# Two stages change places among the first products, the first keys come through a second queue, and the filler multiplies ones

## The chip, the cores and the metric

The kernel runs on one core of a Trainium2 chip. A core has five engines that work at the same time, each with its own queue of instructions: TensorE (matrix products and transposes, PE in the profile; its weight loads are listed as PEld), VectorE (DVE), ScalarE (ACT), GpSimd (POOL) and SyncE (SP), which here only issues transfers between the chip's memory and the core's. The metric is device microseconds (us) from the first to the last instruction; the time of a kernel is the median of its runs.

## The reference

The kernel computes a retention block (attention with decaying weights instead of a softmax) and feeds it to a two-layer network with the activation h * erf(softplus(h)):

```python
B, H, S, D = 8, 8, 576, 64
scores = (q @ k.transpose(0, 1, 3, 2)) / sqrt(D)          # per batch and head
gamma  = 1 - 2.0 ** (-5 - arange(H))
Dmat   = where(i >= j, gamma ** (i - j), 0)                # i query position, j key position
attn   = (scores * Dmat) @ v                               # (B, H, S, D)
x      = attn.transpose(0, 2, 1, 3).reshape(4608, 512)     # tokens x 512

h   = x @ w_in                                             # 4608 x 2048
g   = h * erf(softplus(h))
out = g @ w_out                                            # 4608 x 512
```

The weights come as 64-bit floats and are rounded to 32 bits on the chip; all else is 32-bit floats.

## The kernel before

The 4608 tokens are cut into 36 attention blocks of 128 and into 9 chunks of 512 (four blocks each). Attention block i has three stages, in the text T, S and O with the block's number:

```python
def transposes(i):                       # T: queries and keys, on TensorE through PSUM
    ...
    for name in "qk":
        ...
            pt = ps_at.tile([P, NP, P], FP32, tag="at", name=f"pt_{name}")
            for p in range(NP):
                nc.tensor.transpose(pt[:, p, :], flat(t[name][:, 2 * p : 2 * p + 2, :]), ident)
            ...
                nc.scalar.copy(out=tT, in_=pt)          # ScalarE takes them out of PSUM
    load(i + 2, "q")

def scores(i):                           # S: q k^T, then the mask, on VectorE
    ...
            nc.tensor.matmul(ps[e][:, p, :], lhsT=t["kT"][...], rhs=t["qT"][...], ...)
    for e in range(2):
        tt(sT[:, e], ps[e], mask..., ALU.mult)

def outputs(i):                          # O: masked scores x values, running state; needs sT
    ...
    load(i + 3, "kv")
```

From block 8 on the queries are transposed by VectorE (`raw_qs`), and only the keys go through TensorE and ScalarE. The first chunk's product with w_in is cut into 16 steps, which the loop below calls `p`: for each of four slices of the 512 inputs, four products (tiles p, p, pe, pg), each of which grows over the slices. The last four end with a copy by ScalarE:

```python
def plain(self):
    acc = [ps_a.tile([P, W], FP32, tag="a", name=f"p{n}") for n in range(2)]
    acc += [ps_e.tile([P, W], FP32, tag=n, name="p" + n) for n in "eg"]
    ...
    for dc in range(n_dc):                                  # 4 slices
        for n in range(4):                                  # p, p, pe, pg
            ...
                nc.tensor.matmul(acc[n]..., lhsT=wa[...], rhs=t[...], ...)
            if dc == n_dc - 1:
                nc.scalar.copy(out=(self.t2 if tok else self.t1)[:, f], in_=acc[n])
            yield

def softplus(self): ...    # ScalarE, two activations of 128x1024
def erf(self): ...         # ScalarE, two activations of 128x1024
```

A weight tile arrives in two transfers (w_in) or one (w_out) and is rounded in five steps: two activations on ScalarE (L250, L251), then VectorE (L255, L259, L263, and L268 to L271; for w_out GpSimd takes the last two). Each slice of the products needs one rounded w_in tile.

All engines run in program order. The start of the program is written as one string, a letter a stage: `a` the next attention stage, `p` the next product step, `w` the transfer of a weight tile, a digit that many rounding steps, `k` two filler products, `l`, `c` and `s` transfers. A filler is a product of the identity with itself whose result nobody reads; it keeps TensorE from idling:

```python
idle = ps_e.tile([P, W], FP32, tag="g", name="idle")
def keep_busy(n):
    for _ in range(n):
        nc.tensor.matmul(idle[:, :P], lhsT=ident, rhs=ident, start=True, stop=True)
...
keep_busy(9)
weigh_values(0)
products = firsts[0].plain()
for what in "alkakakawkakakawaa3awwa2aaa5ppappawwppa5ppawapp5wcppa5ppaaapp5s":
    ...
firsts[0].softplus()
firsts[0].erf()
attend(after_chunk(1))                                      # O7
store_x(1)
for step, _ in enumerate(firsts[1].plain()):                # the next chunk's products
    if step % 2 == 0:
        attend(min(done[0] + 1, most[0]))                   # T8, S8, T9, O8, ...
    round_weights(int(step > 1))
    ...
```

Written out from the first product on (pp is two product steps; numbered pp1 to pp8), the string before gives: pp1 T5 pp2 O4 ww pp3 S5 5 pp4 O5 w T6 pp5 5 w c pp6 S6 5 pp7 T7 O6 S7 pp8 5 s, and then softplus, erf, O7.

Of the kernel before, what the change touches and what calls it, by code (L numbers as in the profile page):

```python
# [11 lines left out]
FP32 = mybir.dt.float32  # L12
# [6 lines left out]
P = 128  # L19
# [35 lines left out]
def kernel(  # L55
# [10 lines left out]
    nc = tc.nc  # L66
# [15 lines left out]
    cpool = ctx.enter_context(tc.tile_pool(name="cpool", bufs=1))  # L82
# [21 lines left out]
    heads = [slice(e * D, (e + 1) * D) for e in range(2)]  # L104
# [18 lines left out]
    def load_squares(i, name, src):  # L123
        t = raw.tile([P, NP, P * D // SQ], FP32, tag=name + "s", name=f"raw_{name}s", bufs=2)
        for b, s0, n, r0 in pieces[i]:
            m = n // SQ * D
            for part in range(P // SQ):
                e, d0 = part // 2, part % 2 * SQ
                tokens = src[b, e * NP : (e + 1) * NP, s0 : s0 + n, :].rearrange("p (r a) d -> r p (a d)", r=SQ)
                at = r0 // SQ * D  # L130
                nc.sync.dma_start(
                    out=t[part * SQ : (part + 1) * SQ, :, at : at + m - SQ], in_=tokens[:, :, d0 : d0 + m - SQ]
                )
        return t

    def load_rows(i, name, src, bufs):
        if name == "q":
            t = raw.tile([P, NP, P * D // SQ], FP32, tag="qs", name="raw_q", bufs=bufs)
            t = t.rearrange("p a x -> p (a x)")[:, : H * D].rearrange("p (h d) -> p h d", h=H)
        else:  # L140
            t = raw.tile([P, H, D], FP32, tag=name, name=f"raw_{name}", bufs=bufs)
        for b, s0, n, r0 in pieces[i]:
            for e in range(2):
                heads = src[b, e * NP : (e + 1) * NP, s0 : s0 + n, :]
                nc.sync.dma_start(out=t[r0 : r0 + n, e::2, :], in_=heads.rearrange("h p d -> p h d"))  # L145
        return t

    def load(i, names="qkv"):
        if i < len(pieces):
            t = loaded.setdefault(i, {})  # L150
            for name in names:
                src = {"q": q, "k": k, "v": v}[name]
                if name == "q" and i < SQUARES:
                    t["q"] = load_rows(i, "q", q, 2)
                elif name == "q":
                    t["qs"] = load_squares(i, "q", q)
                    if i >= SQUARES_K:
                        t["ks"] = load_squares(i, "k", k)
                elif name == "v" or i < SQUARES_K or len(pieces[i]) == 1:
                    t[name] = load_rows(i, name, src, 4)  # L160

    load(0)
    cst = cpool.tile([P, CONST_COLS], FP32, name="cst")
    nc.sync.dma_start(out=cst[:, :CONST_FIRST], in_=consts[:, :CONST_FIRST])
# [63 lines left out]
    def load_weights():  # L228
        part = next(coming, None)
        if part is not None:  # L230
            t = wraw.tile([P, 2 * WP], UINT32, tag="wraw", name="wraw")
            for rows, src in part[0]:
                nc.sync.dma_start(out=t[rows].rearrange("p (h f) -> p h f", h=2), in_=src)
            words.append((t, *part[1:]))
# [49 lines left out]
    def round_weights(n=1):  # L284
        for _ in range(n):
            next(round_step, None)

    ident = cpool.tile([P, P], FP32, name="ident")
# [13 lines left out]
    def weigh_values(i):  # L302


        if i < len(pieces) and i not in weighed:
            weighed.add(i)
            t = (loaded.get(i) or live[i])["v"]
            by = gk if len(pieces[i]) == 1 else gk2
            nc.gpsimd.tensor_tensor(out=t, in0=t, in1=by.unsqueeze(2).to_broadcast([P, H, D]), op=ALU.mult)
# [136 lines left out]
    def attend(upto):  # L446
        while done[0] < min(upto, len(stages)):
            of, i = stages[done[0]]
            of(i)
            done[0] += 1  # L450
# [9 lines left out]
    def store_x(c):  # L460
        nc.sync.dma_start(out=xd[c], in_=x[0, c][:, :n_dc])
# [240 lines left out]
    idle = ps_e.tile([P, W], FP32, tag="g", name="idle")  # L702

    def keep_busy(n):
        for _ in range(n):
            nc.tensor.matmul(idle[:, :P], lhsT=ident, rhs=ident, start=True, stop=True)  # L706


    most = [before_chunk(2)]
# [1 line left out]
    def run(steps, rounds=(), stages=1):  # L711

        for step, _ in enumerate(steps):
            attend(min(done[0] + stages, most[0]))
            round_weights(rounds[step] if step < len(rounds) else 0)

    keep_busy(9)
    weigh_values(0)
    products = firsts[0].plain()

    for what in "alkakakawkakakawaa3awwa2aaa5ppappawwppa5ppawapp5wcppa5ppaaapp5s":
        if what == "a":
            attend(done[0] + 1)
        elif what == "p":
            next(products)
        elif what == "s":
            store_x(0)
        elif what == "l":  # L730
            load(2, "kv")
        elif what == "c":
            nc.sync.dma_start(out=cst[:, CONST_FIRST:], in_=consts[:, CONST_FIRST:])
        elif what == "w":
            load_weights()
        elif what == "k":
            keep_busy(2)
        else:
            round_weights(int(what))
# [17 lines left out]
    for b, nxt in zip(blocks[2:], blocks[3:] + [None]):  # L757
        n = order.index((b.g, b.c))
# [73 lines left out]
```

## Time and profile before

| | before |
|---|---|
| time, median of 3 runs | 1032.35 us (1030.36 to 1032.41) |
| span of the profiled execution | 1030.6 us |
| busy: TensorE, VectorE, ScalarE, GpSimd | 1018.5, 666.8, 390.2, 122.4 us |
| granted TensorE clock, mean | 0.998 |
| SyncE issues transfers without a break | 0.73 to 16.72 us |
| first filler, first transposes on TensorE | 1.36, 5.36 us |
| first weight tile: issued, landed | 16.72, 23.5 us |
| ScalarE: table loads, softplus and erf of the first chunk | 60.59 to 67.20 us |

A line of the profile names the engine, the line of the kernel, the operation, the tile written and the tiles read, and the shape; x16 is the number of instructions. In brackets stands how long the engine stood idle before it and what ended the wait. A query of a stretch of time gives, for each engine, the busy time, and beside it the clock that TensorE was granted (1.00 is full speed) and the mean busy share of the 16 DMA engines. [...]

### The profile page before, as it was taken

Reading aid. Unit: us, or ns where it says so; the run is one execution under the profiler, and the core shown is the slowest. Engines: PE = TensorE matmul, PEld = TensorE weight load, DVE = VectorE, ACT = ScalarE, POOL = GpSimd, SP = SyncE. Lnnn points to the kernel's source line nnn. Section 1 sums busy time; section 2 is a strip of 40 time slices with the busy share of each in tenths; the row PEclk is TensorE's granted clock in tenths of the full one; section 3 lists DMA queues with packets and bytes.
Section 4 is the critical chain, followed back from the end, with each engine's and each line's share of the span. In section 5 each row is a group of like instructions: output and inputs, shape, how many; then the busy total and the mean of one; then the engine's idle time right before and its main releaser. Section 6 shows DMA issues by size and latency. Waiting matters only on the chain.

```text
span 1030.6 us, 15945 instructions
## 1 busy us (share of the span) xinstructions
PE 1018.5 (99%) x6346; PEld 877.0 (85%) x6346; DVE 666.8 (65%) x1054; ACT 390.2 (38%) x481; POOL 122.4 (12%) x122
## 2 busy tenths in 40 slices
PE   8989999999999999999999999999999999999998
PEld 7778888888788888888888888888888888888887
DVE  2858877777876666666566666666667655555555
ACT  2354133232244544334343344444443333333332
POOL 2233121222311110000001001100100000000000
PEclk9999999999999999999999999999999999999999
DMA  9996979979984444444445344444433334444433
GB/s 187 210 249 141 238 166 241 236 167 247 225 193 148 165 143 143 143 158 166 160 145 174 138 143 145 159 167 143 143 123 123 123 126 129 131 134 131 125 90 115
DMA packets 146986, 165.76 MB, mean 161 GB/s; under 512 B 97376, under 2 KB 121568, under 8 KB 138848
## 3 DMA queue, kind: packets, MB, share of 16 engines
q1 hardware_dynamic: 145904, 163.96, 56.0%
q8 instruction: 50, 0.82, 0.3%
q10 hardware_dynamic: 1008, 0.79, 0.3%
q14 instruction: 24, 0.20, 0.1%
HBM read 117.52 MB, written 47.19 MB: 160 GB/s over the span
## 4 chain that ended last, share of the span: by engine, by line
PE 95%; DVE 1%; ACT 1%; SPq 1%; DMA 1%; issue 0%; POOL 0%; POOLq 0%; ACTq 0%; DVEq 0%
PE a L600 24%; PE a L492 23%; PE g L600 12%; PE g L492 12%; PE e L600 6%; PE e L492 6%; PE s L343 3%; PE o L361 3%; PE o L384 2%; PE o L372 1%; PE p L546 1%; PE pg L546 1%; SPq L145 1%; DMA wraw<-in_moe_w_in_dram 1%; PE pe L546 1%; PE idle L706 0%
## 5 line engine op out<-in xcount | busy, mean ns | idle before, releaser
L492 PE MATMUL a<-x,wa 128*128 128x256 f32 x1088 | 258.3, 380 | 0.0
L492 PEld LDWEIGHTS a<-x,wa 128*128 128x128 f32 x1088 | 205.7, 190 | 28.5
L600 PE MATMUL a<-wb,s 128*128 128x256 f32 x864 | 205.7, 381 | 0.0
L600 PEld LDWEIGHTS a<-wb,s 128*128 128x128 f32 x864 | 162.9, 190 | 23.6 <-ACT o L614 0.7
L99 DVE TENSOR_TENSOR t<-g,t 128x512 f32<-128x512 f32 x68 | 47.0, 691 | 150.4 <-ACT t L522 113.2
L492 PE MATMUL g<-x,wa 128*128 128x256 f32 x544 | 129.2, 380 | 0.0
L492 PEld LDWEIGHTS g<-x,wa 128*128 128x128 f32 x544 | 102.8, 190 | 14.4
L99 DVE TENSOR_TENSOR o<-a,o 128x512 f32<-128x512 f32 x108 | 74.1, 686 | 49.3 <-PE a L600 49.3
L517 ACT COPY t<-a 128x512 f32<-128x512 f32 x34 | 19.9, 585 | 188.2 <-PE a L492 188.2
L99 DVE TENSOR_TENSOR t<-t,s 128x1024 f32<-128x1024 f32 x72 | 88.4, 1268 | 0.0
L561 ACT ACTIVATE s<-t 128x1024 f32<-128x1024 f32 x72 | 72.1, 1049 | 27.4 <-DVE t L99 27.4
L270 POOL TENSOR_TENSOR wraw<-wraw 128x512 f32<-128x512 f32 x28 | 29.4, 1051 | 443.3 <-DVE wraw L268 185.9
L99 DVE TENSOR_TENSOR x<-x 128x512 f32<-128x512 f32 x115 | 75.7, 692 | 1.2
L528 ACT COPY t<-a 128x512 f32<-128x512 f32 x34 | 19.9, 586 | 144.3 <-PE a L492 144.3
L565 ACT ACTIVATE s<-s 128x1024 f32<-128x1024 f32 x72 | 72.1, 1048 | 0.4
L99 DVE TENSOR_TENSOR sT<-s,cst 128x512 f32<-128x512 f32 x72 | 46.1, 681 | 35.4 <-PE s L343 35.4
L600 PE MATMUL g<-wb,s 128*128 128x256 f32 x288 | 68.6, 381 | 0.0
L600 PE MATMUL e<-wb,t 128*128 128x256 f32 x288 | 68.5, 380 | 0.0
L600 PE MATMUL a<-wb,t 128*128 128x256 f32 x288 | 68.5, 380 | 0.0
L600 PE MATMUL g<-wb,t 128*128 128x256 f32 x288 | 68.2, 380 | 0.0
L99 DVE TENSOR_TENSOR o<-g,o 128x512 f32<-128x512 f32 x72 | 49.2, 684 | 24.8 <-ACT o L614 20.0
L492 PE MATMUL e<-x,wa 128*128 128x256 f32 x272 | 64.8, 381 | 0.0
(75 smaller groups left out, 1226.0 us busy)
## 6 DMA issues: line engine op xcount, KB each, us to landing
od<-o SPq DMA_DIRECT2D x54, 512.0 KB, 3.3
x<-xd SPq DMA_DIRECT2D x27, 1024.0 KB, 4.8
o<-od SPq DMA_DIRECT2D x27, 1024.0 KB, 5.2
raw_qs<-in_q_dram SPq DMA_DIRECT2D x96, 112.0 KB, 4.5
raw_ks<-in_k_dram SPq DMA_DIRECT2D x84, 112.0 KB, 4.3
xd<-x SPq DMA_DIRECT2D x9, 1024.0 KB, 5.1
raw_k<-in_k_dram SPq DMA_DIRECT2D x64, 128.0 KB, 4.6
raw_v<-in_v_dram SPq DMA_DIRECT2D x64, 128.0 KB, 4.6
```

The costliest lines, as they stand in the source:

```text
L99: nc.vector.tensor_tensor(out=out, in0=in0, in1=in1, op=op)
L270: engine.tensor_tensor(out=r_f, in0=high_f, in1=r_f, op=ALU.mult)
L343: nc.tensor.matmul(ps[e][:, p, :], lhsT=t["kT"][heads[e], p, :], rhs=t["qT"][heads[e], p, :], start=True, stop=True)
L361: nc.tensor.matmul(o[p % 2][heads[(e + p) % 2], p // 2, :], lhsT=t["v"][:, 2 * p + e, :], rhs=t["sT"][:, e, p, :], start=(p < 2), stop=(no ...
L384: nc.tensor.matmul(kv[heads[e], p, :], lhsT=t["k"][:, 2 * p + e, :], rhs=t["v"][:, 2 * p + e, :], start=False, stop=(p == NP - 1), skip_gr ...
L492: nc.tensor.matmul(acc[:, j * TH : (j + 1) * TH], lhsT=weights["wa", self.g][:, a, d, j * P : (j + 1) * P], rhs=x[self.g, self.c][a][:, d, :],
L517: nc.scalar.copy(out=self.t1[:, 1], in_=self.a)
L528: nc.scalar.copy(out=self.t2[:, 0], in_=self.a)
L546: nc.tensor.matmul(acc[n][:, j * TH : (j + 1) * TH], lhsT=wa[:, slots[f], dc % 2, j * P : (j + 1) * P], rhs=t[:, dc, tok * TH : (tok + 1) ...
L561: nc.scalar.activation(self.s[:, j], t, AF.Softplus)
L565: nc.scalar.activation(self.s[:, j], self.s[:, j], AF.Erf)
L600: nc.tensor.matmul(acc[:, tp, :], lhsT=left[:, j * TH + tp * P : j * TH + (tp + 1) * P], rhs=weights["wb", self.g][:, b, j, :], start=(sta ...
```

## The change

It has three parts. The first pair of transfers of keys is issued by ScalarE, beside the queries on SyncE's queue, so that SyncE's queue is two issues shorter. The filler multiplies a tile of ones that VectorE writes, which does not have to wait for GpSimd's identity, and there are ten at the start instead of nine. And two stages change places in the string: T6 moves from before pp5 to behind it, and pp8 moves from behind O6 and S7 to ahead of them, so that the last products of the first chunk, and with them its copies and its softplus, come earlier.

```diff
         for b, s0, n, r0 in pieces[i]:
             for e in range(2):
                 heads = src[b, e * NP : (e + 1) * NP, s0 : s0 + n, :]
-                nc.sync.dma_start(out=t[r0 : r0 + n, e::2, :], in_=heads.rearrange("h p d -> p h d"))
+
+                queue = nc.scalar if (name, i) == ("k", 0) else nc.sync
+                queue.dma_start(out=t[r0 : r0 + n, e::2, :], in_=heads.rearrange("h p d -> p h d"))
@@
+    ones = cpool.tile([P, P], FP32, name="ones")
+    nc.vector.memset(ones, 1.0)
     load(0)
@@
-            nc.tensor.matmul(idle[:, :P], lhsT=ident, rhs=ident, start=True, stop=True)
+            nc.tensor.matmul(idle[:, :P], lhsT=ones, rhs=ones, start=True, stop=True)
@@
-    keep_busy(9)
+    keep_busy(10)
@@
-    for what in "alkakakawkakakawaa3awwa2aaa5ppappawwppa5ppawapp5wcppa5ppaaapp5s":
+    for what in "alkakakawkakakawaa3awwa2aaa5ppappawwppa5ppapp5wawcppa5ppappaa5s":
```

Written out, the string after gives: pp1 T5 pp2 O4 ww pp3 S5 5 pp4 O5 pp5 5 w T6 w c pp6 S6 5 pp7 T7 pp8 O6 S7 5 s, and then as before.

## The prediction

> **What bounds the kernel now.** I read the page first, then the clock of the core, the waits of TensorE, the timeline of the first 85 us, and the chain of waits over the same stretch. The page says where a gain can be at all:
>
> ```profile
> PE 1018.5 (99%) x6346; PEld 877.0 (85%) x6346; DVE 666.8 (65%) x1054; ACT 390.2 (38%) x481; POOL 122.4 (12%) x122
> PE 95%; DVE 1%; ACT 1%; SPq 1%; DMA 1%; issue 0%; POOL 0%; POOLq 0%; ACTq 0%; DVEq 0%
> ```
>
> TensorE is busy in 1018.5 of 1030.6 us and is 95% of the chain that ended last. So only some 12 us of idle time, and time in which TensorE is busy but slow, can be taken away. What the change edits runs in the first 60 us, so I looked for both there and just behind. The list of TensorE's waits has a single large one:
>
> ```profile
> PE s L343 <- ACT kT L334: 3.6, 2, 3.4
> PE p L546 <- DVE wa L271: 1.1, 1, 1.1
> PE pt_k L328 <- DMA raw_k<-in_k_dram: 0.6, 1, 0.6
> ```
>
> The columns are the total in us, how often, and the longest. The timeline shows what stands before the 3.4 us (columns: start, duration, engine, line, operation):
>
> ```profile
> 56.80 0.73 PEld L546 LDWEIGHTS pe<-x,wa 128*128 128x128 f32 x4
> 57.97 0.58 ACT L555 COPY t<-pe 128x512 f32<-128x512 f32 x1 [3.70 <-PE pe L546]
> 58.84 0.59 ACT L555 COPY t<-pg 128x512 f32<-128x512 f32 x1 [0.28 <-PE pg L546]
> 59.32 0.68 ACT L250 ACTIVATE wb<-wraw 128x512 f32<-128x512 f32 x1
> 59.90 0.68 ACT L251 ACTIVATE wraw<-wraw 128x512 f32<-128x512 uint32 x1
> 60.59 1.28 ACT L561 ACT_TABLE_LOAD   x1
> 61.89 2.00 ACT L561 ACTIVATE s<-t 128x1024 f32<-128x1024 f32 x2
> 63.91 1.28 ACT L565 ACT_TABLE_LOAD   x1
> 65.20 2.00 ACT L565 ACTIVATE s<-s 128x1024 f32<-128x1024 f32 x2
> 67.11 0.56 ACT L334 COPY kT<-pt_k 128x512 f32<-128x512 f32 x1
> 67.73 1.30 PEld L343 LDWEIGHTS s<-qT,kT 64*128 64x128 f32 x16 [3.79 <-ACT kT L334]
> ```
>
> The reader is to see an unbroken ScalarE queue from 58.84 to 67.67 us. The transposed keys of attention block 8 wait in PSUM from about 62.5 us, but their copy stands behind two table loads, softplus and erf, and those behind the copies of the last two products of the first block (pe, pg). The scores of block 8 (L343) wait for that copy. The granted clock of the same microseconds shows a second cost (columns: stretch, its length, TensorE busy, clock, DMA share, GB/s):
>
> ```profile
> 66.00:67.00 1.00, 0.00 (x0) 1.00 0.97 402
> 67.00:68.00 1.00, 0.27 (x4) 1.00 0.97 410
> 68.00:69.00 1.00, 1.00 (x16) 0.65 1.07 286
> 69.00:70.00 1.00, 1.00 (x6) 0.50 1.35 238
> 70.00:71.00 1.00, 1.00 (x4) 0.50 1.34 345
> 71.00:72.00 1.00, 1.00 (x4) 0.65 0.97 410
> ```
>
> After that idle time TensorE runs at half clock from about 68.3 to 71.7 us: 3.4 us that do 1.7 us of work.
>
> **What the Trainium skill says.** "TensorE: Matmul & The Clock Gate", section "Part 1: The HAM clock gate", puts the clock at half after about one idle window of 3.4 us, and back at full after about 3.4 us of sustained work, with windows that run free of the kernel's start. The trace agrees: 3.39 us idle, then 3.4 us at half. The same page, under "Architectural detail: the array is 16× 32×32, not 1× 128×128", says that ScalarE and VectorE take their queues strictly in order; the copy that stands 4.6 us behind ready data (62.5 to 67.1) agrees. "DMA: Bandwidth & Descriptors", section "Issuing engines are not separate DMA queues", says that transfers issued by two engines share the same 16 DMA engines, and that a second issuer saves only issue time. In this trace one issue takes SyncE 0.5 us, and the DMA share is already 0.91 at 3.0 to 4.5 us and 1.13 at 4.5 to 6.0, so I expect little from the second queue.
>
> **The change part by part.** I write O for an attention block's outputs, S for its scores, T for its transposes, and pp1 to pp8 for the pairs of products; the number after O, S and T is the block.
>
> *Part 1, order, first half.* T6 moves from before pp5 to behind it. Before, O5 ends at 44.02, T6 follows, pp5 begins at 44.77, just behind VectorE's last rounding step for its weights (L271 at 43.99, 0.69 long, so 44.68). Without T6 ahead TensorE waits 44.68 - 44.02 = 0.7 us. The work between 44.02 and pp7 (T6, pp5, pp6, S6) took 43.95 to 49.58 = 5.63 us and only changes its order, so pp7 can begin at 44.77 + 5.63 = 50.40 instead of 50.68. Its weights must be ready: ScalarE's step for them (L250, at 45.65 behind T6's copies) is now ahead of those copies; VectorE starts behind O5's three multiplications (end 45.67), and needs the 3.59 us of the part before (41.09 to 44.68), so 49.3. The wait of 1.1 us at pp7 goes, one of 0.7 comes: gain 0.3.
>
> *Part 2, order, second half.* pp8 moves from behind O6 and S7 to ahead of them. pp7 50.40 + 1.99 = 52.39; T7 0.88 gives 53.27; pp8 1.94 gives 55.2; O6 2.24 and S7 1.09 give 58.53. Now O7 follows S7 at once, and needs the masked scores: two VectorE multiplications, 1.29 us together, so 58.53 + 1.29 and 0.12 of hand-over, 59.94; pp8 used to hide them. Before, O7 began at 58.73 without waiting, so O7 is now 1.2 us later, and so is everything up to the next chunk's third product (its end was 64.34): 65.55.
>
> ScalarE meanwhile: pg's copy ends at about 55.85 instead of 59.43. Then the same queue as in the fence: 1.26 (L250, L251), 1.28, 2.00, 1.28, 2.00, so erf ends at 63.7; block 8's transposes, also 1.2 us later, end at 63.7 too; their copy ends at 64.3. TensorE reaches S8 at 65.55 and finds it ready. The wait of 3.39 becomes none: S8 begins at 65.55 instead of 67.73, gain 2.2 (part 1's 0.3 is in it). No idle stretch longer than 1.3 us is left, so the clock stays up, and S8, pg and p take 1.09 + 1.06 + 0.86 = 3.0 us as their like do elsewhere, instead of the 72.44 - 67.73 = 4.7 measured: gain 1.7. Together 3.9 us at the transposes of block 9.
>
> *Part 3, the first keys on ScalarE's queue.* It takes two issues, 1.06 us, out of SyncE's queue, which issues without a break from 0.73 to 16.72, and the first weights (issued at 16.72, landed at 23.5) end a wait in the chain. At most 1.06 us, if SyncE alone set the pace; DMA shares of 1.17 to 1.23 from 7.5 to 15 us say that the transfers set it too, while 0.62 and 0.67 at 15.0 to 16.5 and 18.0 to 19.5 leave room. I choose half: 0.5 us. Queries and keys now come in together; the first transposes start at 5.36, behind the filler, and do not need either earlier.
>
> *Part 4, the filler.* It begins at 1.36 now, once GpSimd has built the identity. A tile of ones needs one VectorE memset and should be ready about 0.4 us earlier. One more product (two instructions of 4.21 / 18 = 0.234 us) takes 0.47. It ends where it ended: 0 us, unless the clock rises a window earlier.
>
> Sum: 3.9 + 0.5 = 4.4 us, if all of it reaches the end.
>
> **The rivals.** (a) *The gain is given back later.* DMA is at a share of 1.03 in 150 to 200 us, and at 272 us the chain goes through a transfer of keys (2.68 us) for 0.6 us of TensorE's waiting. If transfers, and not TensorE, set the pace up to 300 us, an earlier TensorE only waits longer, and 2 to 4 us are lost: 1029 to 1032. Against it: the loads are issued as buffers come free, which moves earlier too, and slices with a DMA share of 0.6 and 0.7 lie between. (b) *The wait for masked scores at O7 takes the place of the one removed*, and the clock falls anyway: with a wait of 2 us or more and softplus not hidden, S8 would gain 1 us or nothing: 1030 to 1032. Against it: VectorE's queue is empty at that point, its rounding steps stand behind the masking. (c) *Part 1 costs more than it gains*: if pp5's weights come 1 us later than worked out, 0.7 us is lost. (d) *Queries and keys in two queues delay the first transposes* (the queries alone had landed by about 4.1 us): they have 1 us of slack, so 0 to 0.5 us. (e) SyncE's queue was the bound and all of 1.06 comes through: 1027.4.
>
> **Range and chances.** 1032.35 - 4.4 = 1028.0. For rival (a) I take 0.3 off the gain in the mean: 1028.3. The three times of before spread over 2.05 us (1030.36 to 1032.41), about the cost of one fall of the clock, so a median can lie 1 us off; the full gain with (e) and a lucky start gives 1026.2, most of (a) or (b) gives 1031.3. A change of 2% is 20.6 us; TensorE's total idle time is 12, so faster by that is not to be had, and nothing here could cost as much: 0.99 for within 2%.
>
> **What would show each step.** ScalarE's copies of pe and pg at about 54 to 56 us; the wait of L343 for kT gone from TensorE's list, and a wait of O7 (L361) for VectorE's sT of 1 to 1.5 us in its place; granted clock 1.00 in all of 60 to 80 us; TensorE's wait at the first pp5 instead of pp7; block 9's transposed keys at 68 us or earlier instead of 72.4; SyncE's first weight transfer issued at 16.2 instead of 16.7. I am wrong if TensorE still waits over 2 us before S8, if the clock still falls there, or if block 9 is 4 us earlier and the end is not.

## The result, and the profile after

| | before | after |
|---|---|---|
| time, median of 6 runs | 1032.68 us (1030.36 to 1033.56) | 1027.33 us (1026.85 to 1029.08) |
| span of the profiled execution | 1030.6 us | 1026.7 us |
| ratio, with 95% interval | | 0.9953 (0.9940 to 0.9966) |

A ratio of 0.9953 is 4.9 us less, with an interval of 3.5 to 6.2. The two profiled executions differ by 3.9 us. The page of the changed kernel, busy time of the engines and the chain that ended last:

```profile
PE 1017.5 (99%) x6348; PEld 876.0 (85%) x6348; DVE 669.2 (65%) x1055; ACT 390.2 (38%) x481; POOL 123.5 (12%) x122
PE 95%; DMA 2%; DVE 2%; SPq 0%; issue 0%; ACT 0%; DVEq 0%
```

TensorE remains the bound. It is busy 1.0 us less, although the first filler takes 4.64 us instead of 4.21: here the half clock that is gone shows. The other 2.9 of the 3.9 us were idle time. TensorE's waits of the changed kernel in the first 100 us (the columns are the total in us, how often, and the longest; line numbers are four higher than before):

```profile
PE idle L710 <- DVE ones L165: 1.1, 1, 1.1
PE o L365 <- POOL raw_v L313: 0.8, 1, 0.8
PE p L550 <- DVE wa L275: 0.7, 1, 0.7
PE pt_k L332 <- DMA raw_k<-in_k_dram: 0.7, 2, 0.4
PE s L347 <- ACT kT L338: 0.3, 1, 0.3
PE pt_q L332 <- DMA raw_q<-in_q_dram: 0.2, 1, 0.2
```

The wait of 3.4 us for the copy of block 8's keys has gone. A wait at the outputs (L365) and waits for transfers of keys and queries stand there instead. Behind 100 us one more is listed, for VectorE's transposes of block 31:

```profile
PE s L347 <- DVE kT L326: 0.9, 1, 0.9
```

The kernel before waits 0.6 us at that place. The timeline of the changed kernel around the scores of block 8:

```profile
54.93 0.61 ACT L559 COPY t<-pe 128x512 f32<-128x512 f32 x1
55.41 0.62 ACT L559 COPY t<-pg 128x512 f32<-128x512 f32 x1
...
57.19 1.28 ACT L565 ACT_TABLE_LOAD   x1
57.95 1.29 DVE L99 TENSOR_TENSOR sT<-s,cst 128x512 f32<-128x512 f32 x2 [0.25 <-PE s L347]
58.71 0.19 PEld L365 LDWEIGHTS o<-sT,raw_v 128*64 128x64 f32 x2 [0.99 <-POOL raw_v L313]
...
59.29 0.85 PEld L365 LDWEIGHTS o<-sT,raw_v 128*64 128x64 f32 x14 [0.39 <-DVE sT L99]
...
61.81 2.00 ACT L569 ACTIVATE s<-s 128x1024 f32<-128x1024 f32 x2
...
63.72 0.57 ACT L338 COPY kT<-pt_k 128x512 f32<-128x512 f32 x1
...
64.75 0.97 PEld L347 LDWEIGHTS s<-qT,kT 64*128 64x128 f32 x16 [0.33 <-issue]
...
68.05 0.42 PEld L332 LDWEIGHTS pt_k<-ident,raw_k 128*128 128x128 f32 x4 [0.62 <-issue]
```

ScalarE's copies of pe and pg come about 3 us earlier, so erf ends at 63.8 and the keys' copy at 64.3, before TensorE has got to block 8's scores (64.75, where it was 67.73). O7 waits for its masked scores: its first two weight loads run at 58.71, the other 14 at 59.29, when VectorE has written sT. The lists put the first part of this wait down to GpSimd (raw_v L313), but that ended at 58.21; VectorE's first half of sT ended at 58.64. The granted clock in the stretch that ran at half before:

```profile
68.00:69.00 1.00, 0.92 (x7) 1.00 1.25 405
69.00:70.00 1.00, 1.00 (x6) 1.00 0.97 410
70.00:71.00 1.00, 1.00 (x15) 1.00 0.92 330
```

The clock stays at 1.00. The most useful view is one worked out from these timelines: when TensorE begins the scores of each attention block, less the same of the kernel before (us; less is earlier). The later columns are experiments told below; S15 to S26 stand as S11 in every column.

| scores of block | before, at | after | order alone | pp8 alone | T6 alone | start alone | filler in the wait | copy first |
|---|---|---|---|---|---|---|---|---|
| 1 | 13.90 | -0.97 | +1.64 | -0.76 | -0.29 | -0.87 | -0.08 | -0.83 |
| 4 | 29.64 | -1.42 | +0.72 | -0.89 | -0.77 | -0.92 | -0.77 | -1.46 |
| 5 | 38.69 | -0.36 | +0.86 | -0.44 | -0.40 | -0.32 | -0.30 | -0.67 |
| 7 | 55.71 | +1.05 | +2.27 | +1.29 | -0.72 | -0.38 | -0.29 | -0.73 |
| 8 | 67.73 | -2.98 | -1.76 | -2.74 | -0.71 | -0.37 | -0.27 | -4.03 |
| 9 | 78.11 | -4.17 | -3.39 | -4.36 | -0.65 | -0.40 | -1.89 | -5.52 |
| 11 | 96.91 | -4.17 | -3.39 | -4.36 | -0.65 | -0.40 | -1.89 | -5.52 |
| 30 | 267.09 | -4.17 | -3.39 | -4.37 | -0.66 | +0.18 | -1.90 | -5.24 |
| 31 | 276.59 | -3.81 | -3.99 | -4.64 | -1.00 | -0.41 | -2.45 | -5.23 |
| 35 | 314.94 | -3.82 | -4.02 | -4.64 | -1.00 | -0.44 | -2.45 | -5.23 |

The column "after" shows where the time is gained. Block 7's scores are later, as pp8 (1.94 us) now stands ahead of them. Between blocks 7 and 9 the lead grows by 5.2 us, these 1.94 included, and what is there at block 9 is still there at block 30.

The first rows need care, since each column is one execution. The columns "pp8 alone", "T6 alone" and "filler in the wait" have the start of the kernel before, yet they too lead by 0.8 to 0.9 us at block 4 and by 0.3 to 0.4 at block 5: the profile of before began late, and the lead of 0.36 at block 5 can't be put down to the new start. Counting from block 5's scores to block 11's leaves the start out: 58.22 us before, 57.97 with T6 alone, 54.30 with pp8 alone, 53.97 with both ("order alone"), and 54.41 and 53.98 in two profiles of the changed kernel.

### The profile page after: what moved, and what is told of

The parts are those of the page before. It is cut to its first block, busy times and chain, and to the rows that moved or that the text cites. A ratio compares the mean times of both kernels' runs of the same rounds, so it can differ in the third digit from the quotient of the medians.

```text
span 1026.7 us, 15951 instructions
## 1 busy us (share of the span) xinstructions
PE 1017.5 (99%) x6348; PEld 876.0 (85%) x6348; DVE 669.2 (65%) x1055; ACT 390.2 (38%) x481; POOL 123.5 (12%) x122
## 3 DMA queue, kind: packets, MB, share of 16 engines
q10 hardware_dynamic: 2064, 1.05, 0.4%
## 4 chain that ended last, share of the span: by engine, by line
PE 95%; DMA 2%; DVE 2%; SPq 0%; issue 0%; ACT 0%; DVEq 0%
PE a L604 24%; PE a L496 23%; PE g L604 12%; PE g L496 12%; PE e L604 6%; PE e L496 6%; PE s L347 3%; PE o L365 3%; PE o L388 1%; PE o L376 1%; DMA raw_k<-in_k_dram 1%; PE p L550 1%; PE idle L710 1%; DMA wraw<-in_moe_w_out_dram 1%; PE pg L550 1%; PE pe L550 1%
```

## The experiments

**Does the order do it, and which half?** Three kernels with the old queue and the old filler: both moves, only pp8, only T6.

```diff
-aaa5ppappawwppa5ppawapp5wcppa5ppaaapp5s     before
+aaa5ppappawwppa5ppapp5wawcppa5ppappaa5s     order_only
+aaa5ppappawwppa5ppawapp5wcppa5ppappaa5s     pp8_only
+aaa5ppappawwppa5ppapp5wawcppa5ppaaapp5s     t6_only
```

> The kernel before with the new order of stages alone (old queue for the keys, old filler). Theory A (order brings nearly all): 3.9 us faster than before, block 8's scores start near 65.5 us, granted clock 1.00 from 60 to 80 us. Theory B (the start brings a good part): 2 to 3 us faster.

Measured: 1028.16 us (1027.60 to 1029.32) against 1032.17; ratio 0.9966 (0.9954 to 0.9978), so 3.5 us faster (2.3 to 4.7). The scores of block 8 began at 65.97 us, and the clock was 1.00 from 60 to 80. Theory A holds: this time alone would leave room for Theory B, but the scores and the clock are as Theory A has them, and the start alone, below, brings 0.3 us. That TensorE was late up to block 7 has a cause of its own in this profile: the clock came up early, at 4 us; TensorE then waited 1.0 us for block 1's queries, and the clock fell again. The rise is read from the number of filler instructions in a microsecond, 7 and then 10, since the clock column says 1.00 from the start on. These are windows of the profile of order_only:

```profile
3.00:4.00 1.00, 1.00 (x7) 1.00 0.81 184
4.00:5.00 1.00, 1.00 (x10) 1.00 1.02 229
...
12.00:13.00 1.00, 1.00 (x9) 0.50 1.28 224
13.00:14.00 1.00, 1.00 (x14) 0.50 1.23 209
```

> Only pp8 moves ahead of O6 and S7; T6 stays before pp5. Theory A: the wait of 3.4 us and the fall of the clock go, O7 waits 1.2 us for the masked scores instead: 3.6 us faster than before. Rival (the two moves only work together, as pp7's late weights hold pp8 back): under 2 us.

Measured: 1027.71 us (1027.45 to 1028.62); ratio 0.9964 (0.9951 to 0.9976), 3.7 us faster (2.5 to 5.1). Block 9's scores are 4.36 us earlier, of which 0.4 were there at block 5 and are not the order's doing, as the stages up to there are the same. The moved pp8 is nearly the whole effect of the order: 3.9 us between blocks 5 and 11, where both moves together have 4.25. Its waits:

```profile
PE p L546 <- DVE wa L271: 1.1, 1, 1.1
PE o L361 <- POOL state L423: 0.8, 1, 0.8
...
PE s L343 <- ACT kT L334: 0.2, 1, 0.2
```

The wait of 1.1 us for pp7's weights stays, and does not hold pp8 back enough to matter; the rival falls.

> Only T6 moves behind pp5; pp8 stays behind S7. Theory A: the wait of 1.1 us before pp7 becomes one of 0.7 before pp5, and everything behind it, ScalarE's chain too, shifts: 0.3 us faster, the wait of 3.4 us and the half clock stay. Rival: 0.7 us slower, if pp5's weights are the bound and pp7's are not.

Measured: 1032.52 us (1031.36 to 1034.36); ratio 1.0007 (0.9999 to 1.0015), so between 0.1 us faster and 1.5 slower. Its profile has the waits as expected:

```profile
PE s L343 <- ACT kT L334: 3.6, 2, 3.4
...
PE p L546 <- DVE wa L271: 0.7, 1, 0.7
```

and a lead that grows by 0.3 us between blocks 5 and 8 (0.40 to 0.71). A second pair of profiles agrees: from block 5's scores to block 8's, pp8 alone takes 26.74 us and both moves 26.42. The time does not show that gain; if anything it leans the other way. For the end its sign stays open.

**Does the start bring anything?** The two parts of the start together, and each alone, with the old order.

```diff
+queue = nc.scalar if (name, i) == ("k", 0) else nc.sync     # queue_only, start_only
+nc.vector.memset(ones, 1.0)                                 # filler_only, start_only
-keep_busy(9)
+keep_busy(10)
```

> Keys of block 0 on ScalarE's queue and the filler of ones, old order of stages. Theory A: 0.4 us faster at the end, as the transfers of block 5's queries and keys take back about 1 of the 1.4 us that the first product gains; the wait of 3.4 us and the half clock stay. Theory B: 1.5 us faster or more.

Measured: 1031.92 us (1029.80 to 1033.39) against 1032.17; ratio 0.9997 (0.9988 to 1.0006): 0.3 us, from 1.2 faster to 0.6 slower. The wait of 3.4 us and the half clock are there. Theory B falls; whether Theory A's 0.4 us is there the interval leaves open.

> Only the first keys on ScalarE's queue. Theory A: the first weight tile lands about 1.2 us earlier than the 23.5 us of before, the first product starts about 1.2 earlier than 30.75, block 5's keys take that back by 33 us; at the end 0.3 us faster. Rival (the filler is what moves the start): first product within 0.3 us of before.

Measured: 1032.68 us against 1032.56; ratio 0.9998 (0.9990 to 1.0006). The first product began at 29.71 us, 1.04 earlier than before, and the scores of block 5 were 0.15 earlier. But three of the four other profiles with the old start have the first product at 29.84 to 29.96 us.

> Only the filler of ones, ten instead of nine. Theory A: first filler at 1.05 instead of 1.36 us, first transposes within 0.2 us of before, first product within 0.3 us of 30.75; 0 at the end. Rival: the clock rises earlier and the first product starts 1 us earlier.

Measured: 1032.38 us against 1032.56; ratio 0.9998 (0.9989 to 1.0006). The first filler ran at 1.05 us, the first transposes at 5.38, the first product at 30.19, 0.56 earlier, which is more than the 0.3 expected but within what profiles of the old start show; at block 5 0.06 are left. In this profile the first transposes took 0.60 us instead of 1.06, which says that the clock had come up sooner. That is not shown to be the filler's doing: with the same filler they took 1.06 us in fill_t31, and with the old filler 0.60 in order_only.

Taken together, the seven profiles with both parts of the new start (start_only, the changed kernel twice, and the four below that build on it) have the first product at 29.24 to 29.81 us (the middle one 29.31), the five with the old start (before, order_only, pp8_only, t6_only, and the next experiment's) at 29.84 to 31.45 (29.96). So the start brings it forward by some 0.65 us; which part does it is not shown. At block 5's scores the middles are 38.20 and 38.39, and the two groups overlap: most of the gain has been taken back. In the profile of the changed kernel one sees how: the first weights are on ScalarE at 22.15 instead of 23.58 us, and then:

```profile
29.32 1.59 PEld L550 LDWEIGHTS p<-x,wa 128*128 128x128 f32 x8
...
31.56 0.63 PE L332 MATMUL pt_q<-ident,raw_q 128*128 128x128 f32 x4 [0.24 <-DMA raw_q<-in_q_dram]
...
32.60 0.42 PEld L332 LDWEIGHTS pt_k<-ident,raw_k 128*128 128x128 f32 x4 [0.65 <-PE pt_q L332]
32.63 0.63 PE L332 MATMUL pt_k<-ident,raw_k 128*128 128x128 f32 x4 [0.44 <-DMA raw_k<-in_k_dram]
```

The product is 1.43 us earlier than the 30.75 of before, and the transposes of block 5 wait for their queries and then for their keys. The chain of waits puts 6.40 us on that transfer of keys (26.09 to 32.49), after SyncE had issued it 1.5 us sooner than before. From 21 to 24 us the DMA share was 1.25, where it was 1.06 before: the transfer asked for earlier was under way longer, 6.4 us from issue to landing instead of 4.8.

**Wait or clock?** The kernel before with 11 filler products in TensorE's wait; their result is not read.

```diff
     for step, _ in enumerate(firsts[1].plain()):
+        if step == 2:
+            spare = ps_at.tile([P, NP, P], FP32, tag="at", name="spare")
+            for _ in range(11):
+                nc.tensor.matmul(spare[:, 0, :], lhsT=ident, rhs=ident, start=True, stop=True)
```

> The kernel before, with 11 filler products (some 3 us) put into TensorE's wait ahead of block 8's scores; their result is not read. Theory A (the 3.9 us are a wait of 2.2 and 1.7 of half clock): the scores still start near 67.7 us, but the clock stays at 1.00 and the transposes of block 9 come near 70.7 instead of 72.4 us: 1.7 us faster than before. Rival (the half clock costs nothing, as VectorE or the transfers would hold TensorE anyway): 0.

Measured: 1030.10 us (1029.66 to 1032.11) against 1032.56; ratio 0.9975 (0.9967 to 0.9983), 2.6 us faster (1.8 to 3.4). TensorE's timeline, and its clock:

```profile
63.91 2.62 PE L749 MATMUL spare<-ident 128*128 128x128 f32 x22
67.46 1.16 PE L343 MATMUL s<-qT,kT 64*128 64x128 f32 x16 [0.94 <-ACT kT L334]
...
70.38 0.60 PE L328 MATMUL pt_k<-ident,raw_k 128*128 128x128 f32 x4
```

```profile
68.00:69.00 1.00, 1.00 (x14) 1.00 1.03 434
69.00:70.00 1.00, 1.00 (x7) 1.00 0.94 324
```

The scores of block 8 start where they started (0.27 earlier, which was there at block 7), since the copy they wait for is no earlier. From there to block 9 the lead grows by 1.62 us: products that nobody reads save that time by keeping the clock up. The rival falls. The time says more, 2.6 us. A likely reason is that the fall cost less in the profile of before than in other executions. In the profile of filler_only, which has the same gap, the half clock lasted from about 66.7 to 73.5 us, and from block 8's scores to block 9's it took 11.57 us, against 10.38 before and 8.76 here. The mean clock, listed for each execution, agrees: of 82 executions of the kernel before, four had 1.000 and took 1029.44 to 1030.63 us, 1030.2 on average; the 78 others, at 0.996 to 0.999, took 1032.7 on average. The kernel with the products in the gap, with its median of 1030.10, is as fast as those four.

**Is it the place in ScalarE's queue, and nothing else?** The kernel has the start of the changed kernel and the old order of stages; erf is issued one step later, behind the copy of block 8's keys.

```diff
     firsts[0].softplus()
-    firsts[0].erf()
     ...
     for step, _ in enumerate(firsts[1].plain()):
         if step % 2 == 0:
             attend(min(done[0] + 1, most[0]))
         round_weights(int(step > 1))
-        if step == 4:
+        if step == 1:
+            firsts[0].erf()
+        elif step == 4:
             firsts[0].multiply()
```

> The first keys on ScalarE's queue and the filler of ones, the old order of stages, and erf of the first chunk put behind the copy of block 8's keys in ScalarE's queue. Theory (the wait of 3.4 us is that copy standing behind erf in the queue, and nothing else): softplus ends near 63.5 us, the copy follows, block 8's scores start near 64.1 us without O7 having waited for its masked scores; clock 1.00; block 9's transposes near 67.2; 5 us faster than before. Rival (erf, 3 us later, then holds VectorE's multiplications and with them the later stages): block 8's scores come early, but TensorE waits again before 90 us, and the gain is 3 us or less.

Measured: 1026.98 us (1026.31 to 1027.78) against 1032.23; ratio 0.9947 (0.9933 to 0.9961), 5.5 us faster (4.0 to 6.9). ScalarE's queue, and the scores:

```profile
61.17 2.00 ACT L565 ACTIVATE s<-t 128x1024 f32<-128x1024 f32 x2
63.08 0.56 ACT L338 COPY kT<-pt_k 128x512 f32<-128x512 f32 x1
63.66 1.28 ACT L569 ACT_TABLE_LOAD   x1
64.95 2.00 ACT L569 ACTIVATE s<-s 128x1024 f32<-128x1024 f32 x2
...
63.70 1.16 PE L347 MATMUL s<-qT,kT 64*128 64x128 f32 x16
...
66.73 0.63 PE L332 MATMUL pt_k<-ident,raw_k 128*128 128x128 f32 x4
```

Moving the copy ahead of a table load and erf removes the wait without moving a product, O7 keeps pp8 ahead of it and does not wait, and block 9's scores are 5.5 us earlier than before (0.7 of it was there at block 5). TensorE has no other wait above 0.2 us from there to block 27. The rival falls.

**Can O7's wait be filled too?** The changed kernel with the next chunk's first two product steps between S7 and O7 (they read blocks 4 and 5 only), and later stages one step later.

```diff
+    ahead = firsts[1].plain()
+    next(ahead)
+    next(ahead)
     attend(after_chunk(1))
     store_x(1)
-    for step, _ in enumerate(firsts[1].plain()):
-        if step % 2 == 0:
+    attend(done[0] + 1)
+    for step, _ in enumerate(ahead, 2):
+        if step % 2 == 1:
```

> The changed kernel, with the first two product steps of the next chunk (they need blocks 4 and 5 only) put between S7 and O7, and the later attention stages one step later. Theory A: the wait of 1.2 us at O7 goes; block 8's scores start at 64.4 us with one product step more behind them, so 1.2 us faster than the changed kernel, 5.6 faster than before. Rival (the keys of block 9, landed at 68 us, are the next bound): block 9's transposes still start near 68 us and the gain is 0.9 or less.

Measured: 1027.27 us (1026.45 to 1028.92) against 1032.56; ratio 0.9950 (0.9937 to 0.9962). O7's wait went, but a new one of 0.43 us came, at the next chunk's pe, for ScalarE's erf, and block 8's scores began at 64.87 us, not 64.4. Block 11's scores were 5.04 us ahead of before, 0.87 more than in the changed kernel: Theory A's 1.2 was missed, and the figure is the rival's, though TensorE had no wait for block 9's keys. Then 0.7 of the lead went between blocks 26 and 29 and 0.9 at block 31, where it was 3.42, below the changed kernel's 3.81. So it was run again beside the changed kernel, with a third in which VectorE's transposes of block 31 stand ahead of its two multiplications:

```diff
             run(nxt.first(), (1,) if n > 1 else ())
+            if done[0] < len(stages) and stages[done[0]] == (transposes, 31):
+                transposes(31)
+                early.add((transposes, 31))        # attend() leaves it out later
             f.multiply()
```

> The changed kernel once more, beside the next two. 4 to 5 us faster than before; block 9's scores some 4.2 us ahead of the kernel before, block 31's some 3.8.

> The changed kernel with the next chunk's first two product steps between S7 and O7, once more. Theory (VectorE's order at block 31 gives back what is gained): block 11's scores 0.9 us ahead of the changed kernel's, block 31's level with it or behind; time level with it. Rival (the level times of the first run were chance): 0.9 us faster than the changed kernel at the end too.

> The same, and VectorE's two transposes of block 31 stand ahead of its two multiplications of 128x1024 instead of behind. Theory: the wait of 0.9 us before block 31's scores goes, their lead stays near 4.5 to 5 us over the kernel before, and the kernel is 0.9 us faster than the one without this swap. Rival (the keys of block 31 are in transfer until then): the wait stays, or moves to the multiplications' readers; no gain.

| | us, median | ratio to before (1032.60 us) | lead at block 11 | 30 | 31 |
|---|---|---|---|---|---|
| changed kernel again | 1027.57 | 0.9948 (0.9936 to 0.9960) | 4.76 | 4.76 | 5.36 |
| products ahead of O7 | 1027.33 | 0.9946 (0.9934 to 0.9958) | 5.45 | 5.46 | 4.53 |
| and block 31's transposes first | 1027.50 | 0.9947 (0.9935 to 0.9960) | 4.89 | 4.90 | 4.98 |

VectorE and TensorE near block 31 in the first run of the filled kernel, and VectorE in the last kernel:

```profile
261.04 1.11 DVE L326 STREAM_TRANSPOSE kT<-raw_ks 128x512 f32<-128x512 f32 x1 [1.40 <-DMA raw_ks<-in_k_dram]
...
267.96 3.49 DVE L99 TENSOR_TENSOR t<-t,s 128x1024 f32<-128x1024 f32 x2
...
272.00 1.04 DVE L326 STREAM_TRANSPOSE kT<-raw_ks 128x512 f32<-128x512 f32 x1
...
273.19 1.16 PE L347 MATMUL s<-qT,kT 64*128 64x128 f32 x16 [0.88 <-DVE kT L326]
```

```profile
267.95 1.11 DVE L326 STREAM_TRANSPOSE kT<-raw_ks 128x512 f32<-128x512 f32 x1
268.89 2.34 DVE L99 TENSOR_TENSOR t<-t,s 128x1024 f32<-128x1024 f32 x2
```

The changed kernel came out 5.4 us faster than before (4.1 to 6.6), where 4 to 5 was expected, and its leads at blocks 9 and 31 are larger than the 4.2 and 3.8 expected. The filled kernel is level with it in time and behind it at block 31, as its theory has it. With the transposes first the wait at block 31 is gone: the keys were there, so the rival (keys still in transfer) falls, and VectorE's order is what made TensorE wait. But the changed kernel, run again, had no wait there either and led by 5.36. The filled kernel loses 0.9 us at block 31 in both its profiles, the changed kernel lost 0.36 in one and gained 0.6 in the other. Between blocks 5 and 11 all three filled profiles take 53.67 us, only 0.3 less than the 53.98 of the changed kernel's second profile, which had no wait for block 9's keys. The three times lie within 0.24 us of each other with intervals of 2.5 us: the gain of 0.9 us expected of fill_t31 over fill_o7b was not seen, and no one of these, copy_first included, can be told from the changed kernel by its time.

## Why the prediction was right

- **The bound.** As read: the wait of 3.4 us and the half clock behind it are what the change takes away. No other gain at the end is shown.
- **Part 2, pp8 ahead of O6 and S7.** Right in mechanism and size. O7's wait was put at 1.2 us and is 1.3 in the chain (57.97 to 59.29). Block 8's scores were put at 65.55 us, 65.05 with the 0.5 of the start, and began at 64.75; the 0.3 is mostly that the products and stages before O7 overlap a little at their edges (49.99 to 56.76 is 6.77 us, the sum said 7.05). For the profile from which it was read, the clock's 1.7 us holds: 1.62 measured alone.
- **Why the clock stays up.** The prediction argued that no idle stretch longer than 1.3 us is left. The clock did stay up, but the ground is not safe: in order_only it fell behind waits of 1.0 and 0.6 us, so no idle stretch of some 3.4 us, as the rule quoted in the prediction has it, was needed there. Here the measurement decides. What share of idle time is enough stays open.
- **Block 9's transposes.** Put at 68.56 - 0.5 = 68.06, began at 68.08, but partly for a reason not foreseen: they would have run a quarter microsecond sooner and waited for their keys (0.25 us). The changed kernel's second profile has no such wait: from block 8's scores to block 9's it takes 8.75 us, against 9.19 in the first.
- **Part 1, T6 behind pp5.** The waits are the 0.7 and 1.1 us worked out, and pp7 began at 49.99 us against the 50.40 - 0.36 that the lead at block 5 gives. In time the 0.3 us could not be shown.
- **Part 3, the second queue.** Its 0.5 us at the end is not shown: the two parts of the start together measured 0.3 with an interval across zero, and at block 5 the middles of the profiles are 0.2 apart. SyncE's first weight transfer came at 16.23 us (16.2 predicted), but at 16.24 in pp8_only too, which has the old queue. That most of what the first product gains is lost one block later was not worked out; the halving was a guess.
- **Part 4, the filler.** 0 us predicted, and no gain seen at the end (ratio 0.9998). When the clock comes up differs between profiles with either filler.
- **Rival (a), given back later.** It was feared for 150 to 300 us; there the lead stands unchanged for twenty blocks. It happened at block 5 instead, to the start's gain. At block 31 a lead changes by up to 0.9 us in either direction between these profiles.
- **The sum came near partly by luck.** It said 4.4 us, 4.05 after the shading for rival (a); both lie in the interval of 3.5 to 6.2, which can't tell them apart. The term for the clock, 1.7, came from one execution, and in time keeping the clock up is worth 2.6 (1.8 to 3.4); the 0.5 for the start is not shown. An estimate that is too low and one that may be too high partly cancel.

## What to carry to other kernels

An engine that runs its queue in order can starve another with a short instruction: look for a half-microsecond copy behind a block of activations, and move the copy ahead, or the products that the block waits for earlier; both worked here. Where TensorE stood idle for 3.4 us, the half clock behind the gap cost another 1.6 us in one execution and more in others, so count it too. Follow the lead of one engine over one repeated stage through the whole program: it shows in one column where time is gained, and where it is taken back. And compare several profiles of an unchanged start before crediting a change there: here they differ by more than the change brings.

## What the runs showed of the hardware

- The kernel before, whose profile has a gap of 3.39 us on TensorE and half clock behind it, ran with a mean clock below 1.000 in 78 of 82 executions, and with 1.000 in four. An early rise of the clock can be lost again: in order_only it rose at 4 us, and its profile has 0.50 at 12 to 14 us, behind waits of 1.0 and 0.6 us, with TensorE busy 0.53, 0.46 and 0.37 of the three microseconds from 8 to 11.
- VectorE and GpSimd slow each other. Two multiplications of 128x1024 on VectorE took 3.49 us while GpSimd's L275 ran beside them, and that took 2.15 us; in fill_t31, where the two did not meet, they took 2.34 and 1.30. The Trainium skill's "SBUF — State Buffer", under "SBUF: two separate sides", says that a VectorE operation with two SBUF inputs and a GpSimd operation that reads SBUF lock one pair of ports for a whole instruction, and the other "fully blocks"; the two traces agree.
